# A decode kernel that streams its caches: the second key unit in halves, and the first values behind four key units

## Chip, cores and metric

One core of one Trainium2 chip. The metric is the device time in microseconds (us) of one execution. Every number comes from unmodified hardware runs, or from a profile of one execution of the kernel named.

## The reference, cut to what matters

A one-token decode step. Two query heads share each of 8 key/value heads; the caches hold 65536 positions of 256 bf16 numbers, and every byte of them is read once.

```python
xn = _layernorm(A_x)
q = (xn @ wq)                      # 16 heads of 256
scores = q . k_cache * 256**-0.5   # k_cache, v_cache: 1 x 8 x 65536 x 256, bf16
o = softmax(scores) . v_cache
out = x + o @ wo + small_ffn(xn)   # weights of a few MB
```

The two caches are 537 MB of the 549 MB that are loaded.

## The kernel before

The caches come in *units*: a quarter of a head's keys or values, 8.389 MB each. There are three places (slots) in SBUF for units. Keys use slots 0 and 1 in turn, values use slot 2. Slot 2 first holds the query weights. Some key units come in two *halves* (4.194 MB), each with its own semaphore, so that TensorE can start on one half, and free it, while the other is under way. All these loads are issued by SyncE, in one fixed order, and each waits on SyncE until its slot is free.

```python
NSLOT = 3
U = NPP // SBN               # 4 units to a head
UH = U + 1
HALVED = (0, 2, 3, 4)        # key units loaded in halves
...
semtot = {"half1": 16}                     # unit 1 is whole: the wait for its
items[("k", 1, 1)] = ("half1", 16)         # second half is met by a count that GpSimd posts
...
def k_item(u):
    need = [("FREE", u - 2)] if u >= 2 else ()
    if u >= 2 and u in HALVED:
        need = {0: [("FREEH", u - 2)], 1: need}      # half by half
    slot_item("k", u, u % 2, [("slot%d" % (u % 2), CH), ("half%d" % (u % 2), CH)] if u in HALVED else None, need)

def v_item(t):
    slot_item("v", t, 2, None, [("VFREE", t - 1)] if t else [("QT",), ("R",), ("CONST",)])

item("wq", ...)
for u in range(U - 1):
    k_item(u)
v_item(0)
k_item(U - 1)
k_item(U)
k_item(U + 1)
for t in range(1, NT):
    v_item(t)
    if t + U + 1 < NU:
        k_item(t + U + 1)
...
```

TensorE takes a key unit in 8 sets: transpose 16 rows of keys per partition into PSUM, have VectorE and ScalarE copy them out, multiply with the queries. From unit 4 on it puts the values of an earlier unit between the two halves of a key unit: `keys (first half) of unit u`, `values of unit u - 4`, `keys (second half)`. In the first four units (the head of the run) there are keys alone. "3a" and "3b" below are the halves of key unit 3.

## Time and profile before

| | before |
|---|---|
| median of 3 runs | 1277.64 us (1277.31 to 1277.66) |
| span of the profiled run | 1275.6 us |
| loaded | 549.03 MB, 430 GB/s over the span |
| TensorE busy / VectorE / ScalarE | 75% / 45% / 34% |
| TensorE waited for keys / for values | 58.3 us / 197.1 us |

How to read it: no engine is near full, and TensorE waits for loads. So look at the loads: is the queue ever without work? Note the difference between *issued* (SyncE hands a load to the queue) and *landed* (its semaphore lets TensorE go on): a load can stand in the queue for long between the two.

### The profile page before, as it was taken

Reading aid. Unit: us, or ns where it says so; the run is one execution under the profiler, and the core shown is the slowest. Engines: PE = TensorE matmul, PEld = TensorE weight load, DVE = VectorE, ACT = ScalarE, POOL = GpSimd, SP = SyncE. Lnnn points to the kernel's source line nnn. Section 1 sums busy time; section 2 is a strip of 40 time slices with the busy share of each in tenths; the row PEclk is TensorE's granted clock in tenths of the full one; section 3 lists DMA queues with packets and bytes.
Section 4 is the critical chain, followed back from the end, with each engine's and each line's share of the span. In section 5 each row is a group of like instructions: output and inputs, shape, how many; then the busy total and the mean of one; then the engine's idle time right before and its main releaser. Section 6 shows DMA issues by size and latency. Waiting matters only on the chain.

```text
span 1275.6 us, 23521 instructions
## 1 busy us (share of the span) xinstructions
PE 963.0 (75%) x9744; PEld 629.2 (49%) x9744; DVE 570.8 (45%) x1078; ACT 436.6 (34%) x655; POOL 8.1 (1%) x38
## 2 busy tenths in 40 slices
PE   3899988678777779778778776787777698777664
PEld 3676655445544455445455444554454565444321
DVE  4566554445434455343454344454444544444310
ACT  1455433244322434323333333343332334332300
POOL 2000000000000000000000000000000000000000
PEclk9899998889888889887898888898888988888877
DMA  9999999999999999999999999999999999999998
GB/s 410 425 431 437 436 434 436 432 434 432 436 434 436 432 432 436 434 434 432 434 434 434 434 436 432 432 436 434 436 430 434 434 434 436 434 432 432 425 433 355
DMA packets 12742, 549.20 MB, mean 431 GB/s; under 512 B 1335, under 2 KB 1978, under 8 KB 3386
## 3 DMA queue, kind: packets, MB, share of 16 engines
q1 hardware_dynamic: 12724, 549.03, 99.7%
q8 instruction: 8, 0.13, 0.0%
q14 instruction: 4, 0.03, 0.0%
q10 hardware_dynamic: 6, 0.00, 0.0%
HBM read 549.03 MB, written 0.00 MB: 430 GB/s over the span
## 4 chain that ended last, share of the span: by engine, by line
DMA 80%; PE 17%; issue 1%; ACT 1%; SPq 1%; DVE 1%; ACTq 0%; DVEq 0%
DMA ring<-in_A_v_cache_dram 68%; PE ps_o L421 12%; DMA ring<-in_A_k_cache_dram 7%; DMA kt_all<-in_A_wo_dram 3%; DMA ring<-in_A_wo_dram 2%; PE ps_t L421 2%; PE ps_q L421 1%; PE ps_m L421 1%; ACT kt_all L482 1%; SPq L921 1%; DVE kt_all L480 0%; ACT S_sb L563 0%; DVE kt_all L723 0%; PE ps_s L421 0%; DVE kt_all L826 0%
## 5 line engine op out<-in xcount | busy, mean ns | idle before, releaser
L421 PE MATMUL ps_t<-ident_f,ring 128*128 128x128 f32 x4096 | 589.6, 286 | 80.2 <-DMA ring<-in_A_k_cache_dram 58.3
L480 DVE COPY kt_all<-ps_t 128x1024 bf16<-128x1024 bf16 x768 | 487.1, 685 | 291.6 <-PE ps_q L421 286.8
L421 PEld LDWEIGHTS ps_t<-ident_f,ring 128*128 128x128 f32 x4096 | 453.5, 144 | 231.8 <-issue 133.9
L482 ACT ACTIVATE kt_all<-ps_t 128x1024 bf16<-128x1024 bf16 x256 | 262.2, 1024 | 506.2 <-PE ps_q L421 506.2
L421 PE MATMUL ps_o<-ring,p_sb 128*4 128x512 bf16 x2044 | 179.6, 514 | 201.4 <-DMA ring<-in_A_v_cache_dram 197.1
L421 PEld LDWEIGHTS ps_o<-ring,p_sb 128*4 128x4 bf16 x2044 | 53.6, 102 | 290.2 <-issue 264.0
L421 PE MATMUL ps_q<-kt_all,q_cur 128*2 128x512 bf16 x2056 | 163.8, 395 | 0.4 <-DVE kt_all L480 0.3
L504 ACT ACTIVATE s<-ps_q 98x512 bf16<-98x512 f32 x257 | 151.8, 591 | 1.3 <-PE ps_q L421 1.3
L586 DVE RECIPROCAL rs<-ps_m 128x4 f32<-128x4 f32 x29 | 5.3, 183 | 271.6 <-PE ps_m L421 271.6
L573 ACT ACTIVATE p_sb<-S_sb 128x128 bf16<-128x128 bf16 x64 | 18.9, 307 | 262.0 <-PE ps_o L421 261.7
L421 PEld LDWEIGHTS ps_s<-sel_bf,s 128*128 128x128 bf16 x1032 | 64.5, 98 | 5.2 <-ACT s L504 1.9
L421 PE MATMUL ps_s<-sel_bf,s 128*128 128x8 bf16 x1032 | 63.6, 167 | 1.3 <-ACT s L504 1.3
L639 DVE CAST ob_sb<-ps_o 100x512 bf16<-100x512 f32 x29 | 20.1, 692 | 92.0 <-PE ps_o L421 92.0
L421 PEld LDWEIGHTS ps_q<-kt_all,q_cur 128*2 128x2 bf16 x2056 | 26.4, 79 | 44.3 <-issue 44.3
L421 PEld LDWEIGHTS ps_m<-rowsum,ones_f 128*128 128x128 f32 x58 | 12.4, 266 | 23.5 <-issue 23.5
L482 ACT ACT_TABLE_LOAD x7 | 9.0, 1283 | 21.6 <-PE ps_q L421 21.6
L533 DVE TENSOR_REDUCE m1p<-S_sb (+1 forms) x33 | 13.9, 422 | 4.4
L421 PE MATMUL ps_m<-rowsum,ones_f 128*128 128x4 f32 x58 | 14.9, 327 | 0.0
L531 DVE CAST S_sb<-ps_s 128x256 f32 (+1 forms) x33 | 13.7, 415 | 1.9 <-PE ps_s L421 1.9
L563 ACT ACTIVATE S_sb<-S_sb,negmax 128x512 bf16<-128x512 bf16 x16 | 13.2, 852 | 3.2 <-DVE negmax L557 3.2
L421 PE MATMUL ps_m<-diag,ones_f 2*128 2x2 f32 x58 | 11.2, 260 | 3.8 <-DVE diag L548 0.9
L421 PEld LDWEIGHTS ps_m<-diag,ones_f 2*128 2x128 f32 x58 | 8.7, 187 | 10.6 <-DVE diag L548 10.6
(95 smaller groups left out, 132.9 us busy)
## 6 DMA issues: line engine op xcount, KB each, us to landing
ring<-in_A_k_cache_dram SPq DMA_DIRECT2D x8, 4096.0 KB, 30.4
ring<-in_A_v_cache_dram SPq DMA_DIRECT2D x1, 4096.0 KB, 26.8
ring<-in_A_wq_dram SPq DMA_DIRECT2D x1, 3584.0 KB, 11.3
ring<-in_A_wo_dram SPq DMA_DIRECT2D x1, 2688.0 KB, 28.4
ring<-in_A_v_cache_dram SPq DMA_DIRECT2D x1, 2048.0 KB, 31.4
ring<-in_B_w_gate_dram SPq DMA_DIRECT2D x1, 1568.0 KB, 16.5
ring<-in_B_w_up_dram SPq DMA_DIRECT2D x1, 1568.0 KB, 19.9
ring<-in_B_w_down_dram SPq DMA_DIRECT2D x1, 1568.0 KB
```

Of the source, the lines that this page charges most:

```text
L421: return pe.matmul(*a, **k)
L480: O(e, ("EV", s, m), lambda it: nc.vector.tensor_copy(out=kt[:, :], in_=tb[:, :]), f"ev{m}")
L482: O(e, ("EV", s, m), lambda it: nc.scalar.activation(out=kt[:, :], in_=tb[:, :], func=ACTF.Copy), f"ev{m}")
L504: O("act", ("EVQ", s), lambda it: nc.scalar.activation(out=s2[s % 2][0:QROWS, :], in_=ps_q[0:QROWS, :], func=ACTF.Copy), "evq")
L531: O("dve", ("SCOPY", u), lambda it: nc.vector.tensor_copy(out=S_sb[:, at(it, SBN), :], in_=ps_sn), "sc")
L533: O("dve", ("SMAX", u), lambda it: nc.vector.tensor_reduce(out=m1p[:, :, at(it, 1)], in_=S_sb[:, at(it, SBN), :].rearrange("p n i -> p i n ...
L563: O("act", ("EXP", h, i), lambda it, i=i: nc.scalar.activation(out=S_sb[:, :, i], in_=S_sb[:, :, i], func=ACTF.Exp, bias=negmax[:, i:i + 1 ...
L573: O("act", ("PC", t, c), lambda it: nc.scalar.activation(out=p_sb[:, c, :, :], in_=S_sb[:, n:n + CH, :], func=ACTF.Copy), "pc")
L586: O("dve", ("RS", t), lambda it: nc.vector.reciprocal(out=rs[:, :, :], in_=ps_m[0:P, C_TOT:C_TOT + NH * rep]))
L639: O("dve", ("OB", t), lambda it: nc.vector.tensor_copy(out=ob_sb[0:OROWS, :], in_=ps_o[0:OROWS, :]))
L921: eng.dma_start(fn[0], fn[1]).then_inc(sems[sem], 16)
```

## The change

Its intent: TensorE stood idle for 4 us in front of key unit 1, because that unit came only as a whole. Halved, its first part lands before TensorE is through with unit 0. And the head's four key units come in a row, the first values (which TensorE wants only in unit 4) behind them.

```diff
-    HALVED = (0, 2, 3, 4)
+    HALVED = (0, 1, 2, 3, 4)
@@
-    semtot = {"half1": 16}
-    items[("k", 1, 1)] = ("half1", 16)
+    semtot = {}
@@
-    for u in range(U - 1):
+    for u in range(U):
         k_item(u)
     v_item(0)
-    k_item(U - 1)
     k_item(U)
     k_item(U + 1)
@@
-        O("pool", "z_q", lambda it: v.memset(q_cur[:, :, :], 0.0), "half1", 16)
+        O("pool", "z_q", lambda it: v.memset(q_cur[:, :, :], 0.0))
```

## The prediction

> **What bounds the kernel now.** I read the page first: its busy shares, its slices and its queue table.
>
> ```profile
> PE 963.0 (75%) x9744; PEld 629.2 (49%) x9744; DVE 570.8 (45%) x1078; ACT 436.6 (34%) x655; POOL 8.1 (1%) x38
> ...
> DMA  9999999999999999999999999999999999999998
> GB/s 410 425 431 437 436 434 436 432 434 432 436 434 436 432 432 436 434 434 432 434 434 434 434 436 432 432 436 434 436 430 434 434 434 436 434 432 432 425 433 355
> ...
> q1 hardware_dynamic: 12724, 549.03, 99.7%
> ```
>
> No compute engine is full; the queue that carries all loads is, in every slice. Slices 1 and 2 (31.9 us each) stand below 434 GB/s, so if something is lost in the head, it should be there. The chain that ended last gives landings; I read it second (start, us, what; a piece's end is the landing):
>
> ```profile
> 2.12 49.74 DMA ring<-in_A_k_cache_dram
> ...
> 65.24 35.09 DMA ring<-in_A_k_cache_dram
> ...
> 144.06 24.11 DMA ring<-in_A_v_cache_dram
> ...
> 172.40 34.48 DMA ring<-in_A_v_cache_dram
> ...
> 212.88 32.70 DMA ring<-in_A_v_cache_dram
> ```
>
> Key unit 1 lands at 51.86, the first half of key unit 3 at 100.33, value unit 1 at 168.17, 2 at 206.88, 3 at 245.58. The last two are 38.70 us apart, for one value and one key unit. A unit is two halves of 4096.0 KB (page, part 6), 8.389 MB, so the stream moves 16.777 MB in 38.70 us = 433.5 GB/s: 19.35 us per unit, 9.68 per half. Is the head slower? From key unit 1 to the half of key unit 3 the stream carries 2a, 2b, value 0 and 3a: 20.97 MB, 48.4 us at that rate; measured 48.47. From there to value 1 it carries 3b, 4a, 4b, key 5 and value 1: 29.36 MB, 67.7 us; measured 67.84. So the stream has no gap behind key unit 1: the 410 of slice 0 is the start, and the 425 of slice 1 does not show up as lost landing time (whole packets fall on either side of a slice's edge).
>
> A piece of 35.09 us for a half that needs 9.68 tells the same: it stood some 25 us in the queue. The chain names the releaser of the issue, though the issue was not what delayed the data. Third, the issues of the SyncE queue, from its own timeline:
>
> ```profile
> 35.51 0.33 SPq L921 DMA_DIRECT2D ring<-in_A_k_cache_dram  x1
> 47.82 0.33 SPq L921 DMA_DIRECT2D ring<-in_A_k_cache_dram  x1
> 48.27 0.35 SPq L921 DMA_DIRECT2D ring<-in_A_v_cache_dram  x1
> 65.24 0.33 SPq L921 DMA_DIRECT2D ring<-in_A_k_cache_dram  x1
> 76.66 0.33 SPq L921 DMA_DIRECT2D ring<-in_A_k_cache_dram  x1
> ...
> 122.99 0.33 SPq L921 DMA_DIRECT2D ring<-in_A_k_cache_dram  x1
> 144.06 0.33 SPq L921 DMA_DIRECT2D ring<-in_A_v_cache_dram  x1
> 155.28 0.33 SPq L921 DMA_DIRECT2D ring<-in_A_k_cache_dram  x1
> ```
>
> They are key 2a, 2b, value 0, key 3a, 3b, then key 5, value 1, key 6 (4a at 88.06 and 4b at 99.48 fall in the gap). Each comes when TensorE has freed its place, and 65.24, 76.66, 88.06, 99.48 are 11.41 us apart: TensorE needs 22.8 us for a key unit that the stream brings in 19.35. Last, what TensorE waited for at key unit 1, and its clock just after:
>
> ```profile
> 51.91 1.33 PE L421 MATMUL ps_t<-ident_f,ring 128*128 128x128 f32 x5 [4.04 <-DMA ring<-in_A_k_cache_dram]
> ```
> ```profile
> 52.00:56.00 4.00, 4.00 (x22) 2.82 (x23) 0.78 (x2) 1.06 (x2) 0.00 (x0) 0.50 0.97 418
> ```
>
> TensorE stood idle 4.04 us for a unit that came only whole, and then ran at a clock of 0.50 (the third number from the right). Its first half of unit 1 took 65.24 - 51.9 = 13.3 us instead of 11.41. This is what the change is aimed at.
>
> **What the Trainium skill says.** "DMA: Bandwidth & Descriptors", section "Where 436 GB/s comes from", puts the ceiling of one core's 16 DMA engines at 435 GB/s; the 433.5 above agrees, so there is no faster stream to be had. The same page, "Anatomy of one DMA", says that waits for semaphores sit on the issuing sequencer before dispatch while the DMA engines just drain their queues; the 25 us of queueing agrees. Its "Rules for kernel authors" asks for at least 1 MiB per DMA; a half has 4 MiB, so I expect no loss in rate from halving, and the stretch above, made mostly of halves, ran at 432.7. "TensorE: Matmul & The Clock Gate", Part 1, has the clock fall to half after an idle window of some 3.4 us; the 0.50 after 4.04 us idle agrees.
>
> **The change part by part.**
> Removed: the TensorE wait before key unit 1 (4.04 us) and its slow restart (13.3 - 11.41 = 1.9 us), together 5.9 us. Half 1a should land at 51.86 - 9.68 = 42.2, and TensorE ends unit 0 at 47.9.
> Added: one more load of about 0.4 us of SyncE's issue time, all within the first 3 us, while about 20 us of loads are queued: nothing on the path. A real count takes the place of the one that GpSimd used to post; no instruction of a compute engine is added.
> Moved: value 0 goes behind 3a and 3b. The bytes up to 4a are the same in another order, so 4a, 4b, key 5 and all that follows land where they did, if the queue never runs dry.
>
> I check that by stepping TensorE on from 47.82 by 11.41 per half. It frees 1a at 59.2, 1b at 70.65, 2a at 82.1, 2b at 93.5, 3a at 104.9, 3b at 116.3. Landings follow from 51.86 by 9.68 per half: 2a 61.5, 2b 71.2, 3a 80.9, 3b 90.6, value 0 110.0, 4a 119.7, 4b 129.4, key 5 148.8.
> Each load must be issued before its predecessor has landed: 3a at 59.2 against 71.2 (12 us to spare), 3b at 70.65 against 80.9 (10), value 0 right behind it, at 71.1, against 90.6 (19), 4a at 82.1 against 110.0 (28), 4b at 93.5 against 119.7 (26), key 5 at 116.3 against 129.4 (13; before 122.99, so 6).
> Then TensorE waits for 4a, 116.5 to 119.7, some 3.2 us: most of what was won at unit 1 is paid back here. From the start of unit 4 to the end of value 0 it took 144.06 - 123.2 = 20.9 us before, which now ends at 140.6. Value 1 is issued there instead of at 144.06, against key 5's landing at 148.8: 8 us to spare instead of 4.7. It still lands at 168.2, and TensorE, 3.5 us ahead, waits that much longer for it. TensorE waits 197.1 us for values over the run anyway, about 6 us per unit, so the lead ends there.
> Sum on the end: 5.9 us of TensorE waiting removed, 3.2 and then about 3 waited elsewhere, 0.0 us on the stream. The ending (ordering of loads, 1174.5 to 1275.6) is untouched.
>
> **The rivals.**
> A gain: slices 1 and 2 show (434 - 425)/434 x 31.9 = 0.7 us and 0.2 us below the steady rate. If these were gaps that earlier issues close, the time would be 1276.7. A gain of over 2% (25 us) would have to come from the stream, which has nothing like that. For it speaks only the slice row; against it the landings, which leave 0.1 + 0.1 us.
> A dry queue: four key units in a row with two places for them make the stream depend on TensorE, the slower of the two (22.8 against 19.35 us per unit). Every us by which an issue is late beyond its slack would be lost for good. Tightest are value 1 (8 us), 3b (10), 3a (12). A lower granted clock, as in later turns (0.87 to 0.90), could delay them. But key 6 follows value 1 by 11.22 us, and key 7 follows value 2 by the same 11.22 us (172.40 to 183.62), so half a unit hardly stretches. A restart at half clock at 4a costs 1.9 us of the 8. If it happened after all, 1 to 4 us: 1279 to 1282.
> Value 0 late: it lands at 110.0 instead of 90.6, and TensorE wants it about 15 us after 4a, at 135. 25 us to spare, no wait.
> An order effect in memory, all keys and then values: nothing in the trace speaks for it; key and value stretches run at the same rate.
>
> **Range and chances.** Nothing on the stream changes, so I predict the median of before, 1277.6. The three runs lie within 0.35 us. I allow 1 us down (the slice row) and 1.6 up (a short dry queue, another chip): 1276.4 to 1279.2. Faster or slower by 2% would be 25 us, which no term reaches: 0.01 each.
>
> **What would show it right or wrong.** Right: TensorE goes from unit 0 to unit 1 at 47.9 without a wait and at full clock; issues of keys 11.4 us apart from 35.5 or 47.8 to 116.3, with value 0 between 3b and 4a; a new wait of about 3 us for 4a near 116.5; value 1 issued near 140.6 and landed at 168.2 as before; value landings 38.7 us apart. Wrong: a value 1 that lands more than 0.5 us from 168.2, a slice between 32 and 160 us well below 425 GB/s, or an issue later than its predecessor's landing (a dry queue); or a steady interval other than 38.7, which would mean that the order of loads changes the stream's rate.

## The result, and the profile after

| | before | after |
|---|---|---|
| median | 1277.68 us (6 runs, 1277.31 to 1279.25) | 1277.72 us (6 runs, 1277.38 to 1278.23) |
| ratio, 95% interval | | 0.9998 (0.9985 to 1.0011) |
| span of the profiled run | 1275.6 us | 1275.9 us |
| TensorE busy | 963.0 us | 956.1 us |
| TensorE waited for keys / for values | 58.3 / 197.1 us | 62.1 / 201.6 us |

The time did not move. What moved is inside: TensorE was busy 6.9 us less and waited 8.3 us more for loads.

The page of the changed kernel, the same rows (busy shares, GB/s in 40 slices, queue):

```profile
PE 956.1 (75%) x9744; PEld 627.2 (49%) x9744; DVE 570.5 (45%) x1078; ACT 436.6 (34%) x655; POOL 8.0 (1%) x38
...
GB/s 405 428 438 427 443 431 434 434 434 434 434 431 436 434 436 431 434 436 429 434 436 434 434 434 431 436 434 431 436 431 436 434 431 436 431 434 434 424 431 355
...
q1 hardware_dynamic: 12868, 549.03, 99.7%
```

The queue is as full as it was. The third and fifth slices read 438 and 443 and the fourth 427: above the steady 434 and below it side by side. The landings below show no such loss, so I read these as edges of slices, not as gaps.

The issues of the SyncE queue after the change (start, us; what):

```profile
59.32 0.33 SPq L918 DMA_DIRECT2D ring<-in_A_k_cache_dram  x1
70.72 0.33 SPq L918 DMA_DIRECT2D ring<-in_A_k_cache_dram  x1
71.17 0.35 SPq L918 DMA_DIRECT2D ring<-in_A_v_cache_dram  x1
82.14 0.33 SPq L918 DMA_DIRECT2D ring<-in_A_k_cache_dram  x1
...
116.36 0.33 SPq L918 DMA_DIRECT2D ring<-in_A_k_cache_dram  x1
142.32 0.33 SPq L918 DMA_DIRECT2D ring<-in_A_v_cache_dram  x1
```

They are 3a, 3b, value 0, 4a, then key 5 and value 1. All but value 0 come earlier than before, 3a, 3b and 4a by 5.9 us, key 5 by 6.6, value 1 by 1.7. The chain that ended last shows when the data came (issue, us to landing):

```profile
82.14 37.95 DMA ring<-in_A_k_cache_dram
...
142.32 26.17 DMA ring<-in_A_v_cache_dram
...
172.72 34.47 DMA ring<-in_A_v_cache_dram
```

Half 4a lands at 120.09, value 1 at 168.49 (168.17 before), value 2 at 207.19 (206.88). Value 1 was issued 1.7 us earlier and landed no earlier. It only stood in the queue longer: 26.17 us against 24.11.

TensorE itself at the two places that count, from the timeline (in brackets: idle before, and what ended it), with the granted clock there (third number from the right; the share of its full clock that TensorE was given, 1.00 is all of it):

```profile
48.12 1.06 PE L418 MATMUL ps_t<-ident_f,ring 128*128 128x128 f32 x8 [0.18 <-ACT kt_all L479]
...
120.13 1.97 PE L418 MATMUL ps_t<-ident_f,ring 128*128 128x128 f32 x8 [3.72 <-DMA ring<-in_A_k_cache_dram]
```
```profile
52.00:56.00 4.00, 3.91 (x43) 2.74 (x43) 3.12 (x7) 1.97 (x3) 0.00 (x0) 1.00 0.97 418
120.00:124.00 4.00, 3.87 (x21) 2.69 (x22) 0.69 (x1) 0.86 (x1) 0.00 (x0) 0.50 1.00 428
```

At 48 us there is no wait for data any more, and the clock stays at 1.00. The wait is now at 120 us, in front of 4a: 3.72 us, followed by the same drop of the clock to 0.50. The change moved the hole; it did not close it.

### The profile page after: what moved, and what is told of

Read it like the earlier page. It is cut to its first block, busy times and chain, and to the rows that moved or that the text cites. A ratio compares the mean times of both kernels' runs of the same rounds, so it can differ in the third digit from the quotient of the medians.

```text
span 1275.9 us, 23521 instructions
## 1 busy us (share of the span) xinstructions
PE 956.1 (75%) x9744; PEld 627.2 (49%) x9744; DVE 570.5 (45%) x1078; ACT 436.6 (34%) x655; POOL 8.0 (1%) x38
## 4 chain that ended last, share of the span: by engine, by line
DMA 78%; PE 18%; ACT 2%; issue 1%; DVE 1%; SPq 0%; ACTq 0%; DVEq 0%
DMA ring<-in_A_v_cache_dram 69%; PE ps_o L418 12%; DMA ring<-in_A_k_cache_dram 5%; PE ps_t L418 3%; DMA kt_all<-in_A_wo_dram 3%; DMA ring<-in_A_wo_dram 2%; PE ps_q L418 2%; ACT kt_all L479 2%; PE ps_m L418 1%; SPq L918 0%; DVE kt_all L477 0%; ACT S_sb L560 0%; DVE kt_all L720 0%; PE ps_s L418 0%; DVE kt_all L823 0%
## 5 line engine op out<-in xcount | busy, mean ns | idle before, releaser
L418 PE MATMUL ps_t<-ident_f,ring 128*128 128x128 f32 x4096 | 588.0, 285 | 83.3 <-DMA ring<-in_A_k_cache_dram 62.1
L418 PE MATMUL ps_o<-ring,p_sb 128*4 128x512 bf16 x2044 | 173.6, 500 | 205.9 <-DMA ring<-in_A_v_cache_dram 201.6
L479 ACT ACT_TABLE_LOAD x7 | 9.0, 1283 | 27.6 <-PE ps_q L418 27.6
```

Of the source, the lines that this page charges most:

```text
L418: return pe.matmul(*a, **k)
L479: O(e, ("EV", s, m), lambda it: nc.scalar.activation(out=kt[:, :], in_=tb[:, :], func=ACTF.Copy), f"ev{m}")
```

## The experiments

The theory: the stream of loads is the bound and its queue never runs dry in the head, so neither part of the change can touch the end. Rivals: the two parts are worth something each and cancel; or a lead of TensorE in the head does reach the end, or a lag is made up later. Each group below ran on one chip with runs of the kernel before between them, and every kernel gave a correct result.

### One part at a time

half_only puts value 0 back in its old place:

```diff
 (changed kernel)
-    for u in range(U):
+    for u in range(U - 1):
         k_item(u)
     v_item(0)
+    k_item(U - 1)
     k_item(U)
```

> Key unit 1 in halves, value unit 0 left in its old place (behind key 2b). Theory (the queue of loads never runs dry in the head, so neither part touches the end): 1277.7 us, within 0.5 us of before; no wait of TensorE at 48 us, instead a wait of about 6.6 us for key 3a near 93.6 (3a still lands near 100.3); value 1 lands at 168.2 to 168.5. Rival (the two parts are worth something each and cancel): the half alone is faster by some of the 5.9 us of TensorE waiting it removes, 1272 to 1275.

Measured: 1277.83 us (5 runs), before 1277.42 (9 runs), ratio 1.0006 (0.9992 to 1.0019). The wait appeared where it was expected:

```profile
100.47 0.90 PE L419 MATMUL ps_t<-ident_f,ring 128*128 128x128 f32 x3 [5.86 <-DMA ring<-in_A_k_cache_dram]
```

TensorE gained its 4 us at unit 1 and stood idle for 5.86 us at unit 3. Value 1 landed at 168.27.

move_only is the kernel before with the same lines moved as in the change, and unit 1 whole.

> Value unit 0 behind key 3b, key unit 1 whole. Theory (queue never dry): 1277.7 us, within 0.5 us of before; TensorE still waits 4 us for key unit 1 at 48, none for 3a, ends unit 3 at about 122; slack of key 3a 6 us, of 3b 4 us (issue against its predecessor's landing), key 5 7 us, value 1 about 5 us. Rival (the parts cancel): the move alone is slower by 2 to 6 us, 1280 to 1284.

Measured: 1277.68 us (5 runs), ratio 1.0001 (0.9988 to 1.0015). TensorE waited 4.00 us at 51.91 as before and no more at unit 3; value 1 landed at 168.17. Each part alone is worth nothing within 0.2% (2.5 us), so two effects of 3 us or more that cancel are ruled out.

### Further back with value 0

v0_behind_4b moves value 0 one key unit further back, v0_behind_5 two:

```diff
 (changed kernel; v0_behind_4b)
-    for u in range(U):
+    for u in range(U + 1):
         k_item(u)
     v_item(0)
-    k_item(U)
     k_item(U + 1)
 (v0_behind_5: range(U + 2), and no k_item behind v_item(0))
```

> As the changed kernel, but value unit 0 goes one unit further back, behind key 4b. Theory: slack stays positive everywhere (4a issued at 82 against 90.9, 4b 93.5 against 100.6, value 0 right behind, key 5 116.4 against 129.7), so 1277.7 us within 0.5; TensorE does not wait for 4a at 116.5 any more, the first value block starts near 131.7, value 1 is issued near 137 instead of 142.3 and still lands near 168.3. Rival (TensorE's wait for 4a is what the change paid): faster by up to 3.7 us, 1274.

Measured: 1277.72 us (5 runs), ratio 1.0001 (0.9987 to 1.0015). The wait for 4a is gone, value 1 is issued at 139.12 (expected 137: the first value block ran slow), and the chain shows it landing at 168.17, as ever:

```profile
139.12 29.05 DMA ring<-in_A_v_cache_dram
```

So the 3.7 us in front of 4a cost nothing either. TensorE simply waited 5.86 us for value 1 in place of 2.98.

> Value unit 0 behind key 5: the order past the point where the queue stays full. Theory: key 5 can be issued only at 116.4, when the load before it (4b) has landed at 110.3. With about 2.8 us from an issue on an empty queue to its data's share of the stream (11.3 us from issue to landing of the first load, less its 8.5 us at 433.5 GB/s), the loss is 116.4 + 2.8 - 110.3 = 9 us. Then value 0 lands at about 158 with nothing behind it but loads that wait for its slot and for key 4: value 1 is issued after its block, near 164, for another 7 to 9 us. Together 16 to 18 us, all of it on the end: 1293 to 1296. Rival (a lead or lag in the head is made up by the slack of TensorE later): under 3 us.

Measured: 1297.06 us (4 runs) against 1277.42, ratio 1.0153 (1.0138 to 1.0169): 19.6 us slower. The queue ran dry twice, as the stretches of 8 us show (the last two numbers are DMA share, the mean busy share of the core's 16 DMA engines, and GB/s):

```profile
108.00:116.00 8.00, 7.74 (x82) 5.57 (x80) 5.14 (x10) 4.01 (x7) 0.00 (x0) 1.00 0.05 20
...
156.00:164.00 8.00, 5.36 (x62) 2.09 (x66) 0.18 (x1) 0.31 (x1) 0.00 (x0) 0.59 0.00 0
```

Note the first: TensorE is 97% busy there and every view of the engines looks healthy, yet these 8 us are lost for good, because nothing is being loaded. Value 2 landed at 225.32 instead of 206.88, 18.4 us late, and the end came 19.0 us late in the profiled run. Nothing was made up in over 1000 us.

### How late may a load be?

These hold value 1 back until TensorE has gone through a later set of key unit 4. All needed waits stay; one more is added.

```diff
 (changed kernel; q = 5, 6, 7; hold_set7_before: the same in the kernel before, q = 7)
 def v_item(t):
-    slot_item("v", t, 2, None, [("VFREE", t - 1)] if t else [("QT",), ("R",), ("CONST",)])
+    need = [("VFREE", t - 1)] if t else [("QT",), ("R",), ("CONST",)]
+    if t == 1:
+        need = need + [("T", U * SETS + q, TORD[-1])]
+    slot_item("v", t, 2, None, need)
```

> The changed kernel with the issue of value unit 1 held until TensorE has transposed set 5 of key unit 4: near 147.6 us instead of 142.3, against key 5's landing at 149.1. Theory (only what exceeds the slack counts, and an empty queue needs about 2.8 us before data flows): loss 147.6 + 2.8 - 149.1 = about 1.3 us, 1279.0. Rival (lateness counts one for one, as the chain of waits suggests): 5.3 us, 1283.

> The same, held until set 6: issue near 150.5. Theory: loss 150.5 + 2.8 - 149.1 = 4.2 us, 1281.9. Rival (one for one): 8.2 us, 1286.

> The same, held until set 7, the end of key unit 4: issue near 153.5. Theory: loss 153.5 + 2.8 - 149.1 = 7.2 us, 1284.9; from set 5 to set 7 the end moves by the full 5.9 us of lateness. Rival (one for one from the start): 11.2 us, 1289. Rival (TensorE's slack of 6 us per unit swallows it): 1278.

> The kernel before with the same hold: issue near 155.3, against key 5's landing at 148.8. Theory: loss 155.3 + 2.8 - 148.8 = 9.3 us, 1287.0; the changed kernel's lead of some 2 us in TensorE is then worth those 2 us on the end, which it is not while the queue is full. Rival (the lead is worth nothing in any case): the same time as the changed kernel with this hold.

Measured (4 runs each; before on the same chip 1278.04):

| | median, us | over before | ratio (95%) | issue of value 1 in its profile | landing | later than 168.2 |
|---|---|---|---|---|---|---|
| hold_set5 | 1279.09 | 1.1 | 1.0011 (0.9994 to 1.0028) | 145.53 | 170.21 | 2.0 |
| hold_set6 | 1281.11 | 3.1 | 1.0026 (1.0009 to 1.0043) | 147.95 | 169.94 | 1.7 |
| hold_set7 | 1284.49 | 6.5 | 1.0055 (1.0038 to 1.0072) | 152.19 | 174.34 | 6.1 |
| hold_set7_before | 1287.12 | 9.1 | 1.0075 (1.0059 to 1.0092) | 153.78 | 175.78 | 7.6 |

The times are near those of the theory (expected 1279.0, 1281.9, 1284.9, 1287.0) and far from the rival that counts lateness one for one (1283, 1286, 1289); hold_set7 is also far from the rival of 1278. hold_set5 alone decides little: its interval still contains 1. In the profiled runs TensorE reached the held sets 1.3 to 2.6 us earlier than I had assumed. A likely reason is the clock: at 124 to 128 us it was 0.50 in the changed kernel's profile, from which the expectations of the first three came, and 0.98 to 1.00 in theirs. So those runs must be judged from the issue that they show, and that the medians came so near the expected times is in part luck (the profiled runs of hold_set6, 1279.84, and hold_set7_before, 1285.91, are the fastest of their four). hold_set7, in stretches of 2 us, shows the dry queue, and the chain the landing:

```profile
144.00:146.00 2.00, 2.00 (x22) 1.39 (x21) 1.05 (x2) 0.68 (x2) 0.00 (x0) 1.00 1.14 492
146.00:148.00 2.00, 1.91 (x23) 1.23 (x21) 1.28 (x3) 0.90 (x2) 0.00 (x0) 1.00 0.08 33
148.00:150.00 2.00, 1.91 (x25) 1.76 (x22) 1.77 (x3) 1.51 (x2) 0.00 (x0) 1.00 0.00 0
150.00:152.00 2.00, 2.00 (x24) 1.37 (x23) 1.07 (x4) 0.80 (x1) 0.00 (x0) 1.00 0.00 0
152.00:154.00 2.00, 1.82 (x23) 1.14 (x21) 1.10 (x2) 0.71 (x2) 0.00 (x0) 1.00 1.33 459
```
```profile
152.19 22.15 DMA ring<-in_A_v_cache_dram
```

On an empty queue a unit takes 22.15 us from issue to landing (21.99 in hold_set6, 22.00 in hold_set7_before), of which 19.35 are its own bytes: 2.6 to 2.8 us are fixed. So the rule for a queue that has run empty is: loss = issue + 2.7 or 2.8 - landing of the load before it, where that is positive. Key 5 lands at 168.2 - 19.35 = 148.85. hold_set6: 147.95 + 2.7 - 148.85 = 1.8 (measured 1.7). hold_set7: 152.19 + 2.8 - 148.85 = 6.1 (6.1). hold_set7_before: 153.78 + 2.7 - 148.85 = 7.6 (7.6). These three are no test, because the fixed part was read from the same landings. What tests the rule is that the expectations had 2.8 us, from the very first load, before these runs, and that the two dry spells of v0_behind_5 fit: key 5 at 116.85 + 2.7 - 110.3 = 9.3 and value 1 at 164.61 + 2.7 - 158.5 = 8.8, together 18.1 (measured 18.4).

hold_set5 does not fit: by the rule its issue at 145.53 was in time by 0.6 us, and its value 1 landed 2.0 us late.

```profile
145.53 24.68 DMA ring<-in_A_v_cache_dram
```

The kept trace shows what the rule leaves out. It holds 16 completions for each load (no view prints them), and the landing is only the last of them. In hold_set5 those of key 5 run from 147.06 to 148.91, and 11 of the 16 come before 145.53 + 2.7 = 148.23. So by the time that value 1's own data could come, most of key 5 was through: the stream thins out before the landing.

The last pair shows what the change's lead is worth. With the queue dry, the kernel with the change ends 1287.12 - 1284.49 = 2.6 us earlier than the one without, as one would expect if the lead of its TensorE counts (in the profiled runs it issued value 1 1.6 us earlier). But four runs each don't settle the size: they span 1283.80 to 1286.26 and 1285.91 to 1288.46, and the intervals of the two ratios overlap, so the rival of equal times is not quite excluded. With the queue full the lead is worth nothing.

### What a split costs, and a late start

all_halved loads all 32 key units in halves (27 loads more than the changed kernel).

```diff
-    UH = U + 1
-    HALVED = (0, 1, 2, 3, 4)
+    UH = NU
+    HALVED = tuple(range(NU))
```

> The changed kernel with all 32 key units loaded in halves, 27 loads more. Tests what a further split costs the stream: the changed kernel's value 1 landed 0.3 us later than before's in the one profile of each, with one load and 144 packets more. If that 0.3 us is a cost of a split, 27 more cost 8 us: 1286. If it is scatter of a profile (my theory, since the medians differ by 0.04 us): within 1 us of the changed kernel, 1277 to 1279, and value landings stay 38.7 us apart.

Measured: 1279.69 us (5 runs, 1279.54 to 1280.03), before 1277.82 (9 runs), ratio 1.0014 (1.0001 to 1.0028). Neither number was right: 2 us, not 0 and not 8. The landings of value 1 and value 27, from the chain:

```profile
142.41 26.31 DMA ring<-in_A_v_cache_dram
...
1145.25 31.82 DMA ring<-in_A_v_cache_dram
```

They are 168.72 and 1177.07, 26 intervals of 38.78 us. In the kernel before they are 168.17 and 1174.39, intervals of 38.70. Each interval has one load more, so a load costs the full stream 0.08 us: 27 x 0.08 = 2.2 us. The change's one more load is worth that 0.08 us, under the scatter of the medians.

whole0_after and whole0_before load key unit 0 whole, so that TensorE starts late. The wait for its second half is met in the way in which the kernel before did it for unit 1 (shown for the changed kernel; in the kernel before the count goes on the memset of `kt_all`, and `HALVED = (2, 3, 4)`):

```diff
-    HALVED = (0, 1, 2, 3, 4)
+    HALVED = (1, 2, 3, 4)
-    semtot = {}
+    semtot = {"half0": 16}
+    items[("k", 0, 1)] = ("half0", 16)
-        O("pool", "z_q", lambda it: v.memset(q_cur[:, :, :], 0.0))
+        O("pool", "z_q", lambda it: v.memset(q_cur[:, :, :], 0.0), "half0", 16)
```

> The changed kernel, but key unit 0 whole, so that TensorE starts it some 9.6 us later (32.4) and every release of a key place comes that much later. Theory by slack (issue + 2.8 us against the predecessor's landing): 2b issued near 57.4 against 61.5, 3a near 68.8 against 71.2, 3b near 80.2 against 80.9 in the all-keys stretch, so 3a is 0.4 us and 3b 2.1 us too late; value 1 issued near 147 against 148.8 pushed back by those: loss about 2 to 3 us, 1280. Rival (the all-keys order has no cost of its own): as the kernel before with unit 0 whole.

> The kernel before, but key unit 0 whole. With value 0 between 2b and 3a the releases have 19 us more: 3a near 68.8 against 90.6, 3b 80.2 against 100.3, 4b 103 against 119.7, key 5 near 126 against 129.4, value 1 near 147 against 148.8 (1.0 us too late by the 2.8 us). Theory: loss 0 to 1 us, 1278, so 1 to 2 us faster than the changed kernel with unit 0 whole: the old order is the safer one where TensorE is late in the head. Rival (the halves of unit 0 matter in themselves): 9.6 us slower, 1287.

Measured: whole0_after 1282.43 us (5 runs), ratio 1.0043 (1.0029 to 1.0057); whole0_before 1279.71 us (5 runs), ratio 1.0015 (1.0001 to 1.0028). The order is as expected, and the new order loses 2.7 us to the old one when TensorE is late; both lost 1.7 to 2.4 us more than expected. In whole0_after the loss is in the all-keys stretch, where 3a was issued at 69.34 and 3b at 80.77:

```profile
68.00:76.00 8.00, 7.65 (x83) 5.91 (x76) 5.62 (x9) 4.54 (x6) 0.00 (x0) 1.00 0.95 377
76.00:84.00 8.00, 7.64 (x81) 5.51 (x80) 5.08 (x10) 4.30 (x6) 0.00 (x0) 1.00 0.88 348
84.00:92.00 8.00, 7.83 (x81) 5.76 (x80) 5.99 (x13) 4.13 (x7) 0.00 (x0) 1.00 0.95 406
```

Three stretches of 8 us lie below the steady 434 GB/s, and none has a DMA share near 0: the queue is thin rather than empty. By the rule above, with the landings that this run's completions show (2b at 71.98, 3a at 84.04), 3a would cost 0.1 us and 3b nothing; they cost 2.3 and 1.8 us, and value 1 landed at 173.12, 4.9 us late. This is the same misfit as in hold_set5: a load that is issued while its predecessor's last data are still moving comes late although the rule has it in time.

All 13 kept traces together show where this begins. Of the loads issued between 40 and 155 us, each one issued 4.3 us or more before its predecessor's landing followed it without loss (to 0.05 us). The six that were issued 2.6 to 3.9 us before it came 0.4 to 2.4 us late: 3a, 3b and 2b in whole0_after, key 5 and value 1 in whole0_before, value 1 in hold_set5. Anything later met a dry queue, as above. So the margin needed in these kernels lies at some 4 us, not at 2.7.

No version was found that beats both kernels, and none was to be expected from the order of the loads: from key unit 1 on the stream runs at 433.5 GB/s without a gap. Whether the first loads could start faster was not tried.

## Why the prediction was right

Predicted 1277.6 us with 0.98 for "within 2%"; measured 1277.72. Step by step:

- *The stream is the bound, and it has no gap in the head.* Right. Four orders of the same bytes (before, half_only, move_only, v0_behind_4b) put value 1 at 168.17 to 168.27, and the changed kernel at 168.49.
- *5.9 us of TensorE waiting and slow clock removed at unit 1.* Right: 3a was issued 5.9 us earlier (59.32 against 65.24), and so was 3b.
- *Some 3.2 us paid back in front of 4a.* Right in place. It was 3.72 us, and the restart at half clock, which the prediction only allowed for among its rivals, did come: value 1 was issued at 142.32, not at 140.6.
- *The rest waited in front of value 1.* Right: 2.98 us there instead of 0.93, though the prediction had 3.5 us more, because of that restart.
- *0.0 us on the stream.* Right as far as the runs can tell. By all_halved it is 0.08 us for one more load. "No loss in rate from halving" was a little too strong.
- *The count of slack.* The test "issued before its predecessor has landed" was too lenient. A load needs some 4 us before its predecessor's landing, as the section before shows. Value 1 was issued 148.83 - 144.06 = 4.8 us before it in the old kernel and 149.14 - 142.32 = 6.8 us in the new one, so the real margins are less than 1 us and less than 3 us, not 4.7 and 8. Both are still positive, so the time was not touched, but most of the comfort was not there. That the old kernel stood so near the edge was not foreseen.
- *The rival of a gain* (0.9 us from the slices' row) fell: no run was faster, and the low slices do not show in landings. *The rival of a dry queue* did not come true for this change, and v0_behind_5 and the hold runs show that it is the right thing to fear: of the rivals it is the only one that moved the end (all_halved moved it too, by the cost of 27 more loads).

What stays open: what sets the size of the loss in a near miss. In hold_set5 the median of value 1's 16 completions came 1.0 us late and the last 2.0. A queue that is dry for some of the 16 engines and not for others fits the spread of the completions, but the trace doesn't say which engine a completion belongs to, so that is not shown.

## What to carry to other kernels

When a load queue is full, the question to a reordering is not how long an engine waits but whether any load is issued too late for the queue to stay full: set each load's issue against the landing of the load before it, with a margin. The fixed time of a load on an empty queue (2.6 to 2.8 us here) is too small a margin, because the load before thins out before it lands: here 4.3 us were always enough, and 3.9 us were not. The chain of waits can name a wait of a compute engine as the releaser of a load that then stands in the queue for 25 us; subtract the load's own transfer time before believing it. A lead that one engine gains is worth nothing until it reaches the bound, and a late load costs the end in full, even where all engines look busy.

## What the Trainium skill lacked or had wrong

- "DMA: Bandwidth & Descriptors", section "Anatomy of one DMA", gives a fixed cost of some 2.0 us per DMA for loads issued by GpSimd. For loads of 8.389 MB issued by SyncE on an empty queue the runs show 2.6 to 2.8 us over the transfer at the stream's rate (21.99, 22.00 and 22.15 us from issue to landing).
- The same page, "Rules for kernel authors", asks for at least 1 MiB per DMA and stops there. No page states what one load more costs on a queue that stays full: 0.08 us per load (intervals of 38.78 against 38.70 us in all_halved).
- No page says how early a load must be issued for a full queue to stay full: a load issued 3.4 us before its predecessor landed (hold_set5: 145.53 against 148.91) still landed 2.0 us late, and 4.3 us were enough in every run.
- "TensorE: Matmul & The Clock Gate", Part 1, has the clock fall after an idle window of some 3.4 us, and the window run free. Here it fell to 0.50 after gaps of 4.04 (before) and 3.72 us (after), but also after 1.95 us in hold_set6, and not at once after 3.17 us in hold_set7. So in these runs a gap shorter than 3.4 us was no protection, and a held set came 1.3 to 2.6 us earlier than the changed kernel's profile had led to expect.
